# Nine steps of an attention and gated-MLP kernel moved in a hand-listed order: one small load, one copy, three PE steps and four others of batches 0 and 1

## The chip, the core and the metric

The kernel runs on one NeuronCore of a Trainium2 chip. The core has five engines with instruction queues of their own, each worked off in order: TensorE (PE, matrix products), VectorE (DVE), ScalarE (ACT), GpSimd (POOL) and SyncE (SP), which here only issues DMA transfers. The metric is the device time of one execution in microseconds (us), the median of several runs; less is better.

## The reference, cut to what matters

Eight batches, eight heads, 576 tokens, head size 64. A causal sliding-window attention (window 64) is followed by a gated MLP with a spatial projection over the tokens.

```python
scores = scale * np.matmul(q, k.transpose(0, 1, 3, 2))
mask = (rel >= 0) & (rel < window)                 # rel = query - key, window 64
attn = softmax(np.where(mask, scores, -1e9))
x = (attn @ v) as [batch, token, head * 64]        # 512 columns
h = np.maximum(x @ w_in, 0.0)                      # 1024 columns: u and v halves
v_n = (v - mean) / sqrt(var + 1e-6)                # over the 512 columns of v
v_s = einsum('ts,bsd->btd', w_spatial, v_n) + b_spatial
out = (u * v_s) @ w_out
```

## The kernel before

The whole program is a list of 1117 named steps. The functions `load_steps`, `value_steps`, `att_steps`, `gmlp_steps` and so on only describe the steps; the text `ORDER` says in which order they are issued, on which engine, and which PSUM bank or which buffer of a pool each new tile takes (`S1_0:PE:4:7:1:2` is a step on PE that takes banks 4, 7, 1 and 2). Nothing else orders the work: each engine runs its steps in the order of the text and waits at a step for the steps that it depends on, and for the last readers of the bank or buffer that it takes.

A step's name begins with its kind and goes on with the batch `b` and, behind an underscore, the head group `g` (0 or 1) and a part. The kinds that matter here:

- `ldk`, `ldq`, `ldv`, `ldx`: loads of k, q and v (`ldv0_4` the last 64 tokens of v of batch 0, `ldx0_g` the rest of it). `ldwsp`, `ldwin`, `ldwo`, `ldb`: loads of the weights and the bias. `DQ` issues on SP at once; `DG` also on SP, but only when the last matmul listed ahead of it is done.
- `ck`, `cq`, `cv`, `cx`, `cwsp`, `cwin`, `cwo`: the casts of what was loaded to 16 bit (tiles hk, hq, hv, hx, wnat, win, wout). `tk`, `tq`: 32x32 transposes on DVE.
- `Y0_g` and `F0_gk` bring v of batch 0 into token order (tile hv, by way of PSUM). `sl` and `su` copy hv, shifted by 64 tokens, into the lower and upper half of tile hs; `s4` fills its last 64 tokens from the load. In the later batches they come in two parts, `sl1_0`, `su1_0`, `sl1_1`, `su1_1`.
- `S` scores (64 small matmuls), `E` the exponentials on ACT (`E1_10` and `E1_11` write the first tile e of group 1 of batch 1, `E1_12` and `E1_13` the second), `M` the mask on DVE (`M1_10` needs `E1_10` and `E1_11`; `M1_11` the other two), `Z` row sums, `N` and `n` their reciprocal by logarithm and exponential (tile lz), `P` the product with v (from hv and hs), `X` the scaling of it (tile x). `_r` is the remainder of 64 tokens.
- `W0` to `W4` transpose w_spatial on PE and need all five `cwsp`; `We` copy the results out. `V0a`, `V0b`, `V`: v half of the MLP; `Vr`, `Vb`, `Va` its relu and statistics; `L1`, `L2`, `A` the normalisation; `U`, `Ur` the u half; `G`, `Ge` the spatial product and the gate; `O`, `Oe`, `st` the output.

POOL's casts and copies are split into pieces (`cp`): `ck1_0` on POOL would be three, `su1_0` is two copies of 64x512, `cwo10` is one cast of 128x512.

Of the kernel before, what the change touches and what calls it, by code (L numbers as in the profile page):

```python
# [20 lines left out]
ldq0_1a:DQ:3 D9:PE:0 D10:PE:0 D11:PE:0 ck0_0b:ACT cx0_0:DVE:2 D12:PE:0 D13:PE:0 ldq0_1b:DQ D14:PE:0  # L21
ldk0_1b:DQ Y0_0:PE:0:1:2:3 cq0_0b:POOL F0_00:ACT:0 ldx0_1:DQ D15:PE:4 ck0_1a:POOL:3 tk0_0b:DVE
F0_01:ACT ldwsp0:DQ:4 D16:PE:4 D17:PE:4 ldwsp2:DQ:5 tq0_0a:DVE:1 F0_02:DVE D18:PE:4 tq0_0b:DVE
ldwsp1:DQ:6 ldwin10:DQ:7 ldv0_4:DQ D19:PE:4 F0_03:ACT D20:PE:4 cq0_1a:DVE:1 tk0_1a:DVE:2 D21:PE:4
cq0_1b:POOL tq0_1a:DVE:3 D22:PE:4 cwsp0:POOL ck0_1b:DVE ldwin11:DQ:0 tq0_1b:DVE D23:PE:4 D24:PE:4
D25:PE:4 S0_0:PE:4:5:6:7 E0_02:ACT:0 tk0_1b:DVE E0_03:ACT sl0_0x:ACT:0 E0_00:ACT:1 S0_1:PE:0:1:3:2
E0_01:ACT su0_0x:DVE M0_00:DVE cwin110:POOL ldq1_0:DG:1 cx0_1:ACT:2 E0_10:ACT:2 Y0_1:PE:6:7:4:5
ldk1_0:DG:3 M0_01:DVE Z0_01:PE:0 E0_12:ACT:3 F0_12:DVE E0_11:ACT F0_10:DVE cwin111:POOL
S0_r:PE:3:4:1:6 cwsp4:DVE E0_13:ACT E0_r0:ACT:0 M0_11:DVE ldwin01:DQ:2 Z0_00:PE:2 E0_r1:ACT
M0_10:DVE cwsp1:DVE E0_r2:ACT cwsp3:DVE F0_11:ACT cq1_0:POOL:0 cwsp2:DVE P0_00:PE:3 E0_r3:ACT  # L30
Z0_10:PE:4 N0_01:ACT:0 N0_10:ACT:1 Z0_11:PE:1 F0_13:ACT ldwin00:DQ:5 N0_00:ACT:2 M0_r:DVE P0_01:PE:7
W4:PE:6 W3:PE:0 sl0_1x:DVE cwin011:POOL n0_01:ACT su0_1x:DVE n0_00:ACT N0_11:ACT:3 P0_11:PE:4
n0_10:ACT cwin010:POOL cwin101:DVE Z0_r:PE:5 P0_10:PE:2 We3:DVE n0_11:ACT s40_:DVE X0_00:DVE:1
W1:PE:1 cwin100:ACT W0:PE:0 ldk1_1:DG:4 X0_01:DVE P0_r:PE:3 W2:PE:7 N0_r:ACT:4 cwin001:POOL
X0_10:DVE:2 ldq1_1:DQ:6 We4:DVE V0a_3:PE:5 We0:ACT X0_11:DVE ldb:DQ:7 V0a_2:PE:2 V0a_0:PE:0
ck1_0:ACT:1 We2:DVE tq1_0:DVE:4 V0b_2:PE ldwo0:DQ:0 tk1_0:DVE:5 We1:ACT V0b_3:PE n0_r:ACT V0a_1:PE:6
# [3 lines left out]
U0_4:PE:0 Va0_3:DVE E1_01:ACT ldv1_4:DG ck1_1:POOL:3 Vb0_4:DVE:4 Va0_0:DVE Va0_1:DVE Va0_4:DVE  # L40
cb:POOL tk1_1:DVE:0 U0_3:PE:5 L10:ACT:0 ldk2_0:DG:3 L20:ACT U0_1:PE:6 Ur0_4:ACT:0 A0_2:DVE:0
cq1_1:ACT:2 U0_0:PE:4 cwo00:ACT U0_2:PE:3 ldq2_0:DQ:2 A0_0:DVE:1 A0_4:DVE Ur0_1:ACT:1 Ur0_0:ACT:2
Ur0_3:ACT:3 ldq2_1:DQ:5 A0_3:DVE:2 A0_1:DVE:3 tq1_1:DVE:1 cwo01:POOL Ur0_2:ACT:4 G0_0:PE:1
S1_1:PE:2:7:0:6 M1_01:DVE E1_10:ACT:3 E1_11:ACT Ge0_0:DVE:0 E1_12:ACT:2 G0_3:PE:4 S1_r:PE:5:3:1:2
E1_r0:ACT:1 E1_13:ACT M1_00:DVE cv1_0:DVE:1 M1_10:DVE Z1_01:PE:7 sl1_0:POOL:1 N1_01:ACT:5 Z1_00:PE:0
Z1_10:PE:5 E1_r1:ACT G0_1:PE:6 cwo11:POOL G0_4:PE:7 ldk2_1:DQ:4 Ge0_3:DVE:1 G0_2:PE:4 N1_10:ACT:2
M1_11:DVE Z1_11:PE:3 N1_00:ACT:0 su1_0:POOL n1_10:ACT ldq3_0:DG:7 E1_r2:ACT s41_:ACT ldk3_0:DG:6
n1_00:ACT cv1_1:DVE Ge0_1:DVE:2 su1_1:DVE sl1_1:DVE cwo10:POOL ck2_0:POOL:0 P1_10:PE:5 ldv2_0:DQ:0
ldv2_1:DG N1_11:ACT:1 Ge0_2:DVE:3 P1_11:PE:0 n1_01:ACT n1_11:ACT cq2_1:POOL:1 X1_10:DVE:3 E1_r3:ACT
cq2_0:ACT:3 P1_00:PE:6 ck2_1:POOL:2 P1_01:PE:1 O0_2:PE:4 ldv2_2:DQ X1_00:DVE:0 Oe0_2:ACT:0 O0_0:PE:3  # L50
X1_11:DVE ldv2_3:DG tk2_0:DVE:2 O0_3:PE:5 O0_1:PE:6 Oe0_0:ACT:1 tq2_0:DVE:3 X1_01:DVE Oe0_3:ACT
S2_0:PE:2:0:4:3 Oe0_1:ACT V1_3:PE:5 Ge0_4:DVE:4 E2_00:ACT:3 V1_0:PE:1 tq2_1:DVE:0 E2_02:ACT:2
E2_01:ACT V1_2:PE:6 V1_1:PE:7 M1_r:DVE M2_00:DVE Vr1_3:ACT:5 E2_03:ACT tk2_1:DVE:1 Vr1_0:ACT:6
Vr1_2:ACT:7 P1_r:PE:2 cq3_0:POOL:0 Vr1_1:ACT:0 Z1_r:PE:4 S2_1:PE:0:5:3:1 ldv2_4:DQ U1_3:PE:6
N1_r:ACT:3 n1_r:ACT M2_01:DVE E2_12:ACT:1 Vb1_1:DVE:5 X1_r:DVE:1 E2_10:ACT:0 ck3_0:POOL:3 V1_4:PE:7
E2_13:ACT Ur1_3:ACT:5 Vb1_0:DVE:0 Z2_00:PE:4 Z2_01:PE:3 Vb1_3:DVE:1 Vr1_4:ACT:1 Vb1_2:DVE:2
Va1_3:DVE U1_4:PE:2 N2_01:ACT:4 Vb1_4:DVE:1 U1_1:PE:0 Va1_0:DVE cv2_0:POOL:0 N2_00:ACT:2 Va1_1:DVE
ldq3_1:DG:0 E2_11:ACT U1_2:PE:1 Va1_2:DVE Va1_4:DVE L11:ACT:1 M2_11:DVE M2_10:DVE sl2_0:POOL:0
Ur1_4:ACT:2 L21:ACT ldk3_1:DQ:1 S2_r:PE:6:3:4:5 Ur1_1:ACT:3 A1_4:DVE ldv3_0:DG:1 A1_3:DVE:4
E2_r0:ACT:0 A1_1:DVE:5 Z2_11:PE:2 Oe0_4:ACT:0 A1_0:DVE:6 Z2_10:PE:0 N2_10:ACT:0 A1_2:DVE:7 s42_:ACT  # L60
E2_r1:ACT U1_0:PE:6 G1_1:PE:7 N2_11:ACT:1 ldv3_1:DQ cv2_1:POOL su2_0:POOL Ur1_0:ACT:1 E2_r2:ACT
G1_4:PE:0 tq3_0:DVE:4 Ur1_2:ACT:4 G1_0:PE:3 tk3_0:DVE:5 Ge1_4:DVE:5 ldv3_2:DG ldq4_1:DG:3
Ge1_1:DVE:6 su2_1:POOL sl2_1:ACT ldq4_0:DQ:2 ldv3_3:DQ S3_0:PE:2:6:4:1 E2_r3:ACT Ge1_0:DVE:7
P2_10:PE:0 M2_r:DVE n2_10:ACT P2_00:PE:7 n2_11:ACT n2_00:ACT st0_4:DQ P2_01:PE:5 E3_00:ACT:0
X2_10:DVE:1 st0_0:DQ n2_01:ACT cq3_1:POOL:1 X2_00:DVE:2 E3_01:ACT ldk4_0:DG:5 P2_11:PE:3 X2_11:DVE
ck3_1:ACT:2 ldv4_0:DG:0 G1_2:PE:0 X2_01:DVE Ge1_2:DVE:8 P2_r:PE:2 tq3_1:DVE:0 Z2_r:PE:7 cv3_0:POOL:1
ldv3_4:DQ N2_r:ACT:5 n2_r:ACT E3_02:ACT:3 G1_3:PE:3 tk3_1:DVE:1 V2_1:PE:6 Vr2_1:ACT:4 Vb2_1:DVE:0
V2_2:PE:5 sl3_0:POOL:1 V2_3:PE:0 Vr2_2:ACT:2 Ge1_3:DVE:9 Vr2_3:ACT:3 S3_1:PE:7:4:6:5 X2_r:DVE:0
U2_1:PE:3 E3_03:ACT E3_10:ACT:2 Vb2_2:DVE:1 S3_r:PE:0:2:1:7 M3_00:DVE E3_12:ACT:1 su3_0:POOL
E3_r0:ACT:1 M3_01:DVE E3_13:ACT Vb2_3:DVE:2 V2_4:PE:6 Z3_00:PE:0 M3_11:DVE E3_r1:ACT Z3_01:PE:5  # L70
Ur2_1:ACT:0 V2_0:PE:2 cv3_1:ACT Va2_3:DVE cq4_1:POOL:0 sl3_1:POOL Vr2_0:ACT:1 tq4_1:DVE:2 Va2_1:DVE
Vr2_4:ACT:5 Vb2_0:DVE:0 E3_r2:ACT cq4_0:POOL:3 O1_2:PE:3 Vb2_4:DVE:2 E3_11:ACT E3_r3:ACT Va2_0:DVE
Va2_2:DVE Va2_4:DVE su3_1:POOL U2_4:PE:2 M3_r:DVE N3_01:ACT:3 L12:ACT:0 st0_1:DQ s43_:POOL
ldk4_1:DG:4 Oe1_4:ACT:0 L22:ACT M3_10:DVE ldv4_1:DQ Oe1_2:ACT:1 U2_0:PE:1 U2_2:PE:4 U2_3:PE:7
tq4_0:DVE:3 N3_00:ACT:0 O1_1:PE:5 A2_3:DVE:0 A2_4:DVE ldv4_2:DG Ur2_2:ACT:2 ldv4_3:DQ ldv4_4:DQ
A2_2:DVE:1 O1_3:PE:6 Ur2_4:ACT:3 A2_0:DVE:2 Z3_r:PE:3 A2_1:DVE:3 Z3_11:PE:0 Ur2_3:ACT:1 Ur2_0:ACT:4
P3_00:PE:4 n3_00:ACT Oe1_3:ACT N3_r:ACT:2 Z3_10:PE:2 P3_10:PE:7 X3_00:DVE:0 n3_01:ACT ck4_0:POOL:1
N3_10:ACT:1 P3_01:PE:1 tk4_0:DVE:0 P3_11:PE:6 O1_0:PE:3 G2_0:PE:4 N3_11:ACT:4 ldq6_1:DG:7 n3_10:ACT
G2_3:PE:2 n3_11:ACT cv4_0:POOL:0 n3_r:ACT X3_01:DVE X3_10:DVE:3 Oe1_0:ACT:0 sl4_0:ACT:0 X3_11:DVE
Oe1_1:ACT G2_1:PE:0 ck4_1:ACT:2 S4_0:PE:1:7:3:6 Ge2_3:DVE:0 E4_00:ACT:0 ldk5_0:DQ:6 E4_02:ACT:2  # L80
Ge2_0:DVE:1 V3_1:PE:2 E4_01:ACT Vr3_1:ACT:0 ldk5_1:DG:0 V3_2:PE:5 E4_03:ACT G2_2:PE:4 tk4_1:DVE:1
S4_1:PE:1:3:7:2 s44_:ACT Vr3_2:ACT:6 E4_12:ACT:3 su4_0:POOL U3_1:PE:6 E4_10:ACT:1 ldv5_0:DQ:1
E4_13:ACT st1_4:DQ V3_3:PE:5 E4_11:ACT Ge2_1:DVE:2 Vb3_1:DVE:0 ldq5_0:DG:1 U3_0:PE:0 M4_00:DVE
M4_01:DVE ldq5_1:DG:3 Ge2_2:DVE:3 cv4_1:POOL V3_0:PE:7 M4_11:DVE Vr3_3:ACT:7 G2_4:PE:1 M4_10:DVE
su4_1:POOL Ur3_0:ACT:5 st1_0:DQ Ur3_1:ACT:1 S4_r:PE:4:2:3:5 Vb3_2:DVE:1 Vb3_3:DVE:2 Vr3_0:ACT:3
ldq6_0:DQ:2 E4_r0:ACT:0 sl4_1:POOL ck5_1:POOL:0 E4_r1:ACT ck5_0:POOL:3 Z4_10:PE:0 P3_r:PE:6
Va3_3:DVE P4_10:PE:7 X3_r:DVE:1 Z4_00:PE:4 N4_10:ACT:5 E4_r2:ACT Z4_01:PE:2 n4_10:ACT Ge2_4:DVE:4
N4_00:ACT:0 P4_00:PE:6 ldv5_1:DQ N4_01:ACT:3 ldv5_2:DG P4_11:PE:0 V3_4:PE:3 cq5_0:POOL:1 tk5_1:DVE:4
Z4_11:PE:1 X4_10:DVE:1 n4_00:ACT P4_01:PE:4 U3_4:PE:2 E4_r3:ACT N4_11:ACT:1 Oe2_4:ACT:0 ldv5_3:DG
U3_2:PE:7 tk5_0:DVE:5 U3_3:PE:5 Va3_1:DVE X4_00:DVE:2 Vr3_4:ACT:5 n4_11:ACT Ur3_4:ACT:4 tq5_0:DVE:0  # L90
cq5_1:POOL:2 Ur3_3:ACT:0 O2_2:PE:1 n4_01:ACT S5_0:PE:6:3:2:5 Ur3_2:ACT:2 X4_11:DVE O2_3:PE:0
# [872 lines left out]
```

## Time and profile before

| | |
|---|---|
| runs timed | 199.40, 199.76, 199.78 us |
| median | 199.76 us |
| profiled execution, first to last instruction (span) | 197.1 us |
| what the timed runs have beside that span | 2.3 to 2.7 us |
| mean granted TensorE clock | 0.981 |
| busy: PE, DVE, ACT, POOL | 186.1, 162.7, 161.9, 83.7 us |

The page gives the profiled execution by its span alone; a time of its own, with what lies around the span, is not listed, so it is set against the timed runs as above. Times in the profile count from the start of the span. In a row of the timeline the first number is the start, the second the length of the stretch from the first to the last of its instructions, then engine, line, operation, tiles and count; what stands in square brackets is how long the engine sat idle ahead of it and what ended the wait. "PEclk" or "clock" is the granted share of TensorE's full speed.

### The profile page before, as it was taken

How to read it: one execution, taken by the hardware profiler on the slowest of the kernel's cores; microseconds unless marked ns; L12 is line 12 of the kernel's file. 1: busy time of each engine (PE TensorE's matmuls, PEld its weight loads, DVE VectorE, ACT ScalarE, POOL GpSimd, SP SyncE). 2: the span in 40 equal slices, each digit the busy share in tenths (PEclk: the TensorE clock that was granted, in tenths of full speed). 3: DMA queues.
4: the chain of work that ended last, by engine and by line, in shares of the span. 5: the costliest groups of instructions: out<-in, count | busy, mean ns of one | idle time of the engine just before them, and what ended most of it. 6: DMA issues, size and time to landing. Idle time of an engine off the chain costs nothing.

```text
span 197.1 us, 7044 instructions
## 1 busy us (share of the span) xinstructions
PE 186.1 (94%) x2935; PEld 98.1 (50%) x2935; DVE 162.7 (83%) x321; ACT 161.9 (82%) x342; POOL 83.7 (42%) x148
## 2 busy tenths in 40 slices
...
GB/s 196 386 319 310 389 395 239 277 399 294 125 141 259 232 367 300 152 249 226 266 309 325 303 228 156 118 307 199 191 7 97 172 3 0 30 40 161 135 169 191
DMA packets 46977, 42.67 MB, mean 217 GB/s; under 512 B 34529, under 2 KB 35681, under 8 KB 46946
## 3 DMA queue, kind: packets, MB, share of 16 engines
...
HBM read 32.79 MB, written 9.44 MB: 214 GB/s over the span
## 4 chain that ended last, share of the span: by engine, by line
PE 66%; ACT 19%; DVE 10%; issue 2%; POOL 1%
PE bank L295 66%; ACT e L568 6%; ACT vs L726 3%; ACT ru L828 3%; DVE e L573 2%; DVE x L605 2%; DVE g L859 1%; DVE hs L312 1%; ACT lz L612 1%; DVE vn L799 1%; ACT ob L703 1%; POOL hq L307 1%; DVE st L728 1%; DVE hv L312 1%; DVE qT L433 1%
## 5 line engine op out<-in xcount | busy, mean ns | idle before, releaser
L295 PE MATMUL bank<-wspT,vn 128*128 128x512 f16 (+3 forms) x320 | 43.1, 286 | 0.9 <-DVE vn L799 0.7
L295 PE MATMUL bank<-wout,g 128*128 128x512 f16 (+2 forms) x164 | 39.1, 375 | 0.3 <-DVE x L605 0.2
L295 PE MATMUL bank<-win,x 128*128 128x512 f16 (+1 forms) x160 | 38.6, 380 | 0.2 <-ACT e L568 0.2
L568 ACT ACTIVATE e<-bank 128x512 f16<-128x512 f32 x64 | 35.3, 603 | 3.3 <-PE bank L295 3.2
L295 PE MATMUL bank<-x,win 128*128 128x64 f16 (+1 forms) x256 | 35.0, 286 | 0.0
L859 DVE TENSOR_TENSOR g<-bank,ru 128x512 f16<-128x512 f32 (+1 forms) x40 | 24.1, 623 | 11.7 <-PE bank L295 7.0
L728 DVE BATCH_NORM_STATS2 st<-vs 128x6 f32<-128x512 f16 (+1 forms) x40 | 26.4, 679 | 8.9 <-ACT vs L726 8.7
L310 POOL COPY hs<-hv 64x512 f16<-64x512 f16 x38 | 25.4, 694 | 13.6 <-ACT hv L303 8.1
L295 PEld LDWEIGHTS <-vn 128*128 128x128 f16 (+1 forms) x320 | 20.1, 97 | 20.2 <-DVE vn L799 2.0
L703 ACT COPY ob<-bank 128x512 f32<-128x512 f32 (+1 forms) x39 | 22.9, 593 | 8.2 <-PE bank L295 7.9
L726 ACT ACTIVATE vs<-bank 128x512 f16<-128x512 f32 (+1 forms) x40 | 23.5, 607 | 4.4 <-PE bank L295 4.3
L828 ACT ACTIVATE ru<-bank 128x512 f32<-128x512 f32 (+1 forms) x40 | 21.2, 561 | 3.5 <-PE bank L295 3.4
L573 DVE TENSOR_TENSOR e<-e,mask 128x1024 f16<-128x1024 f16 x32 | 22.4, 720 | 1.7 <-ACT e L568 1.5
L295 PEld LDWEIGHTS <-win 128*128 128x128 f16 x256 | 15.8, 98 | 15.4 <-issue 1.5
L295 PEld LDWEIGHTS <-x 128*128 128x128 f16 (+1 forms) x160 | 14.9, 100 | 16.5 <-issue 0.8
L295 PEld LDWEIGHTS <-g 128*128 128x128 f16 (+1 forms) x164 | 15.0, 100 | 14.5 <-issue 0.4
L605 DVE TENSOR_TENSOR x<-bank,lz 128x512 f16<-128x512 f32 x32 | 20.5, 673 | 1.0 <-ACT lz L614 0.9
L433 DVE STREAM_TRANSPOSE kT<-hk 128x576 f32<-128x576 f32 (+1 forms) x18 | 20.2, 1121 | 1.0 <-ACT hk L303 1.0
L433 DVE STREAM_TRANSPOSE qT<-hq 128x576 f32<-128x576 f32 (+1 forms) x18 | 20.1, 1118 | 0.8 <-POOL hq L307 0.5
L307 POOL CAST hq<-nq 128x384 f16<-128x384 f32 x30 | 14.1, 505 | 14.9 <-DMA nq<-in_q_dram 8.8
L614 ACT ACTIVATE lz<-lz 128x512 f32<-128x512 f32 x32 | 19.9, 649 | 0.0
L307 POOL CAST hk<-nk 128x384 f16<-128x384 f32 x30 | 15.9, 567 | 9.3 <-DMA nk<-in_k_dram 9.2
...
## 6 DMA issues: line engine op xcount, KB each, us to landing
...
ws<-in_moe_w_spatial_dram SPq DMA_DIRECT2D x2, 576.0 KB, 10.2
```

The costliest lines, as they stand in the source:

```text
L295: last[0] = nc.tensor.matmul(*a, **kw)
L307: nc.gpsimd.tensor_copy(o[:, n:n + w], i[:, n:n + w])
L310: nc.gpsimd.tensor_copy(o[:, c, :, :], i[:, c, :, :])
L433: lambda e, cs=cs, j0=j0, j1=j1: nc.vector.transpose(qt.t[:, :].rearrange("p (i j) -> p j i", j=18)[:, j0:j1, :], h.t[:, cs].bitcast(f32). ...
L568: lambda e, u=u, w=w: nc.scalar.activation(e2[u].t[:, w, :], sc[2 * u + w].t[:, :], AF.Exp, bias=0.0, scale=0.125),
L573: mins.append(add(f"M{b}_{g}{u}", ("DVE", 0.65), key, lambda e, u=u: nc.vector.tensor_tensor(e2[u].t[:, :, :], e2[u].t[:, :, :], mask[:, : ...
L605: lambda e, u=u, ob=ob, lz=lz: nc.vector.tensor_tensor(x.t[:, u, :], ob.t[:, :], lz.t[:, :], ALU.mult),
L703: lambda e: (nc.vector.tensor_copy if last else nc.scalar.copy)(view(), m.t[rows, 0:n]),
L726: rl = add(f"Vr{b}_{j}", ("ACT", 0.49), key, lambda e: nc.scalar.activation(vs.t[0:jn, :], m.t[0:jn, :], AF.Relu), deps=[pv], acq=[vs], us ...
L728: s1 = add(f"Vb{b}_{j}", ("DVE", 0.6), key + 0.02, lambda e: nc.vector.bn_stats(st6.t[0:jn, 0:6], vs.t[0:jn, :]), deps=[rl], acq=[st6], us ...
L828: lambda e, m=m, ru=ru, n=n: nc.scalar.activation(ru.t[:, 0:n], m.t[:, 0:n], AF.Relu), deps=[pu], acq=[ru], uses=[m])))
L859: lambda e, m=m, g=g, ru=ru, n=n: nc.vector.tensor_tensor(g.t[:, 0:n], m.t[:, 0:n], ru.t[:, 0:n], ALU.mult),
```

## The change

The steps, engines and instructions stay the same ones. In the list these move:

1. `ldv0_4` from behind `ldwin10` to ahead of `ldwsp0`.
2. `sl0_0x` (ACT) from between `E0_03` and `E0_00` to ahead of `E0_02`.
3. `ldq1_0` and `ldk1_0` (both `DG`) from behind `S0_1` and `Y0_1` to behind `S0_r`; they stay next in SP's own order.
4. `N0_10` (ACT) behind `F0_13` and `N0_00`.
5. On PE, `W3` ahead of `W4`, `W1` ahead of `P0_11`, and `P0_r` ahead of `W0`. Thereby the `DG` load `ldk1_1`, listed behind `W0`, waits for `P0_r` where it waited for `P0_10` (transposes are not counted as matmuls there).
6. `s40_` (DVE) ahead of `cwin101` and `We3`.
7. In batch 1, `E1_12` (ACT) ahead of `E1_11`, and `cwo10` (POOL) ahead of `su1_0`.

Beside it 278 of the 290 PE steps take other banks, and some lz and st buffers are numbered anew. The code gets a helper `wide` that, for a step on PE, issues the same matmul as before, and `out_steps` copies by `cp`, which issues the same copy on the engine that the list names.

```diff
-Y0... F0_01:ACT ldwsp0:DQ:4 D16:PE:4 D17:PE:4 ldwsp2:DQ:5 ... ldwsp1:DQ:6 ldwin10:DQ:7 ldv0_4:DQ
+ldv0_4:DQ F0_01:ACT ldwsp0:DQ:4 D16:PE:4 D17:PE:5 ldwsp2:DQ:5 ... ldwsp1:DQ:6 ldwin10:DQ:7
...
-... E1_10:ACT:3 E1_11:ACT Ge0_0:DVE:0 E1_12:ACT:2 ...
+... E1_10:ACT:3 E1_12:ACT:2 Ge0_0:DVE:0 E1_11:ACT ...
...
+    def wide(e, o, w, x, **kw):
+        if e == "PE":
+            mm(o[:, :], w, x, **kw)
+        else:
+            for f in (0, 64):
+                mm(o[f:f + 64, :], w[:, f:f + 64], x, **kw)
...
-        cpy = add(f"Oe{b}_{j}", ("DVE", 0.4) if last else ("ACT", 0.49), key,
-                  lambda e: (nc.vector.tensor_copy if last else nc.scalar.copy)(view(), m.t[rows, 0:n]),
+        cpy = add(f"Oe{b}_{j}", [("ACT", 0.49), ("DVE", 0.6)], key,
+                  lambda e: cp(e, view(), m.t[rows, 0:n]),
```

SP, the loads of the first microseconds: `ws` are `ldwsp0`, `ldwsp2` and `ldwsp1`, `wi` the w_in loads, the 64x8x64 `nv` is `ldv0_4`. Before:

```order
L489 DMA nv_131<-in_v_dram 128x4x256
L353 DMA ws_200<-in_moe_w_spatial_dram 128x2x576
L358 DMA ws_204<-in_moe_w_spatial_dram 64x576
L353 DMA ws_211<-in_moe_w_spatial_dram 128x2x576
L336 DMA wi_213<-in_moe_w_in_dram 128x2x512
L530 DMA nv_131<-in_v_dram 64x8x64
L336 DMA wi_230<-in_moe_w_in_dram 128x2x512
```

After:

```order
L496 DMA nv_131<-in_v_dram 128x4x256
L537 DMA nv_131<-in_v_dram 64x8x64
L360 DMA ws_201<-in_moe_w_spatial_dram 128x2x576
L365 DMA ws_205<-in_moe_w_spatial_dram 64x576
L360 DMA ws_212<-in_moe_w_spatial_dram 128x2x576
L343 DMA wi_214<-in_moe_w_in_dram 128x2x512
L343 DMA wi_232<-in_moe_w_in_dram 128x2x512
```

The small load went ahead of the three w_spatial loads and one w_in load; the rest keeps its order.

ACT in the middle of batch 1, behind the relus `Ur0` (tile ru): `e_1_10` is the tile that `M1_10` masks, `e_1_11` that of `M1_11`. Before:

```order
L828 ACTIVATE ru_2_845<-bank_70 128x512
L568 ACTIVATE e_1_10_919<-bank_69 128x512
L568 ACTIVATE e_1_10_919<-bank_74 128x512
L568 ACTIVATE e_1_11_924<-bank_67 128x512
L642 ACTIVATE er_965<-bank_72 128x128
L568 ACTIVATE e_1_11_924<-bank_73 128x512
```

After:

```order
L834 ACTIVATE ru_2_845<-bank_74 128x512
L575 ACTIVATE e_1_10_919<-bank_72 128x512
L575 ACTIVATE e_1_11_921<-bank_69 128x512
L575 ACTIVATE e_1_10_919<-bank_71 128x512
L649 ACTIVATE er_965<-bank_68 128x128
L575 ACTIVATE e_1_11_921<-bank_67 128x512
```

The second exponential of tile e_1_10 now comes third instead of second.

POOL in the same stretch: `hs` are the pieces of `sl1_0` (one) and `su1_0` (two), `wout_115` is `cwo10`. Before:

```order
L312 CAST wout_114<-wo_639 128x512
L310 COPY hs_975<-hv_969 64x512
L312 CAST wout_116<-wo_666 128x512
L310 COPY hs_975<-hv_969 64x512 x2
L312 CAST wout_115<-wo_666 128x512
L307 CAST hk_0_1048<-nk_0_800 128x384 x3
```

After:

```order
L319 CAST wout_114<-wo_639 128x512
L317 COPY hs_975<-hv_969 64x512
L319 CAST wout_116<-wo_666 128x512
L319 CAST wout_115<-wo_666 128x512
L317 COPY hs_975<-hv_969 64x512 x2
L314 CAST hk_0_1048<-nk_0_800 128x384 x3
```

Two weight casts now run in a row ahead of the two copies into hs.

265 lines of the change are left out of this document (132 added, 133 removed).

## The prediction

> **What bounds the kernel now.** I read the page first, then the chain of waits in order of time, then the timeline and the table of stretches of the first 48 us, which is all that the change reorders.
>
> ```profile
> span 197.1 us, 7044 instructions
> ...
> PE 186.1 (94%) x2935; PEld 98.1 (50%) x2935; DVE 162.7 (83%) x321; ACT 161.9 (82%) x342; POOL 83.7 (42%) x148
> ...
> PE 66%; ACT 19%; DVE 10%; issue 2%; POOL 1%
> ```
>
> PE is busy for 94% of the span and carries two thirds of the chain; DMA does not stand in it. So a delay that reaches the dense part near 42 us has little to swallow it later, while work saved at the start counts only if what ends last there moves too. The stretches of the start (busy time of PE, PEld, DVE, ACT, POOL, then clock, DMA share, GB/s):
>
> ```profile
> 8.00:12.00 4.00, 2.44 (x72) 1.24 (x70) 4.00 (x9) 1.59 (x4) 1.73 (x3) 1.00 1.06 385
> 12.00:16.00 4.00, 2.33 (x114) 1.74 (x114) 3.13 (x7) 4.00 (x8) 0.67 (x1) 0.94 1.05 307
> 16.00:20.00 4.00, 3.71 (x76) 2.49 (x54) 3.73 (x9) 3.49 (x12) 0.00 (x0) 0.50 1.11 295
> 20.00:24.00 4.00, 4.00 (x65) 2.89 (x64) 3.97 (x9) 3.47 (x8) 1.80 (x4) 0.71 1.01 391
> ```
>
> The DMA engines are busy throughout (share 1.01 to 1.11): loads land as the queue serves them, whenever they were issued. The clock is 0.50 in the third stretch; from 0.94 and 0.71 in its neighbours (0.24 and 1.16 us lost, so 0.5 and 2.3 us at half speed) the slow phase runs from 15.5 to 22.3 us. Where the start ends:
>
> ```profile
> 23.37 1.41 POOL L307 CAST hq<-nq 128x384 f16<-128x384 f32 x3 [0.32 <-DVE wspT L312]
> 24.79 1.15 ACT L303 CAST hk<-nk 128x1152 f16<-128x1152 f32 x1 [1.32 <-POOL hq L307]
> 24.82 1.26 DVE L433 STREAM_TRANSPOSE qT<-hq 128x576 f32<-128x576 f32 x1 [0.52 <-POOL hq L307]
> 27.29 0.80 PE L295 MATMUL bank<-qT,kT 32*64 32x128 f16 x64 [0.25 <-DVE kT L433]
> 28.96 1.41 POOL L307 CAST hk<-nk 128x384 f16<-128x384 f32 x3 [0.36 <-DMA nk<-in_k_dram]
> ```
>
> ACT sat idle 1.32 us ahead of `ck1_0`. The name in the bracket is another tensor's cast; by the code `ck1_0` reads only what `ldk1_0` brings, so I read this as the load landing. DVE (0.52) and PE (0.25) idle there too. This is a wall: work done sooner ahead of it waits at it, and lateness ahead of it is forgiven up to these three amounts. Behind it the chain:
>
> ```profile
> 35.37 0.66 DVE g L859
> ...
> 41.06 0.75 DVE hs L312
> 41.81 0.14 issue
> 41.95 5.43 PE bank L295 x120
> ```
>
> From 35.37 to 41.8 DVE runs without a gap (`Ge0_0` to `sl1_1`), then PE is released for 5.43 us of dense work. A delay of DVE in here is a delay of the kernel.
>
> **The change part by part, first the start.**
>
> ```profile
> 8.31 0.41 DVE L312 CAST hv<-bank 128x256 f16<-128x256 f32 x1
> 10.54 1.08 ACT L568 ACTIVATE e<-bank 128x512 f16<-128x512 f32 x2 [2.41 <-PE bank L295]
> 11.51 0.82 ACT L303 COPY hs<-hv 64x768 f16<-64x768 f16 x1
> 14.51 0.67 POOL L312 CAST wnat<-ws 128x576 f16<-128x576 f32 x1 [3.78 <-DMA ws<-in_moe_w_spatial_dram]
> 17.41 1.34 DVE L312 CAST wnat<-ws 128x576 f16<-128x576 f32 x3
> 18.68 0.42 DVE L646 TENSOR_TENSOR er<-er,maskr 128x512 f16<-128x512 f16 x1
> 18.85 1.50 PE L384 MATMUL bank<-id,wnat 128*64 128x128 f16 x10
> ```
>
> `sl0_0x` (11.51, 0.82 us; the next exponential starts 0.72 later) needs `F0_02`, which ends at 8.72 on DVE, and now fits into ACT's idle 2.41 us. ACT's next six steps come 0.7 us sooner, and `Y0_1`, `S0_r` and the Z and P steps with them.
>
> `ldv0_4` goes past four loads. Its price is read from the microsecond in which its packets ran before (16.75 to 17.75), and the landing of `ldwsp1` from its issue:
>
> ```profile
> DMA packets 549, 0.25 MB, mean 250 GB/s; under 512 B 485, under 2 KB 485, under 8 KB 549
> L353 SPq DMA_DIRECT2D ws<-in_moe_w_spatial_dram x1: 445/445/445, 7.7 to 7.7; - x1
> DMA to landing us min/median/max: 10.2/10.2/10.2
> ```
>
> The 64 large packets of 2 KB there are worth 0.13 MB / 385 GB/s = 0.34 us, so 485 small ones took 0.66 and all 512 take 0.7 us (by bytes alone 0.34; at most the full 1 us). The three w_spatial loads and `ldwin10` land that much later; `ldwin11` and all behind it stay, since what is ahead of them is the same. `ldwsp1` landed at 7.7 + 10.2 = 17.9, just where DVE's `cwsp3` (second of the three at 17.41) began; it and `cwsp2` shift to 18.6 and beyond, and with them `M0_r`, `X0_00` and `X0_01`. PE, which went straight from `P0_01` into the transposes at 18.85, now waits for `cwsp2` until about 19.45. What is left at the wall: DVE 0.7 late against 0.52 idle, +0.2; PE 0.6 late at half clock, of which work pushed behind 22.3 us regains half, so 0.3 against 0.25. The first matmuls of batch 1 come 0.1 to 0.2 late, ACT not at all until `Vr0_4`. Bounds: 0 (the load at its bytes' price) and 0.5 (1 us).
>
> The swaps `W3`/`W4`, `W1`, `P0_r`, `s40_`, `N0_10` keep the count of each engine's work ahead of the V steps and cost nothing by themselves; DVE's and PE's idle above covers them. `ldq1_0` and `ldk1_0` are issued 1 to 2 us later, `ldk1_1` with the SP queue behind it (`ldq1_1`, `ldb`, `ldwo0`) about 1.2 us later, behind `P0_r`. The cover is the backlog of the saturated queue: `ldk1_1`, issued at 21.6, was used only at 28.96. Gone, it would cost what the issue is late, 1.2 us at most. The new banks leave every release ahead of its taker by the same steps; `wide` and `cp` issue the same instructions.
>
> **Batch 1: the two swaps.**
>
> ```profile
> 35.77 1.57 ACT L568 ACTIVATE e<-bank 128x512 f16<-128x512 f32 x3 [0.41 <-PE bank L295]
> 36.55 0.67 DVE L312 CAST hv<-nv 128x1024 f16<-128x1024 f32 x1
> 37.15 0.67 DVE L573 TENSOR_TENSOR e<-e,mask 128x1024 f16<-128x1024 f16 x1
> 37.28 1.01 POOL L310 COPY hs<-hv 64x512 f16<-64x512 f16 x1 [4.65 <-DVE hv L312]
> 38.24 1.85 POOL L312 CAST wout<-wo 128x512 f16<-128x512 f32 x1
> 40.16 0.61 POOL L310 COPY hs<-hv 64x512 f16<-64x512 f16 x1
> 40.23 0.81 DVE L312 COPY hs<-hv 64x1024 f16<-64x1024 f16 x1
> 40.71 0.81 POOL L310 COPY hs<-hv 64x512 f16<-64x512 f16 x1
> 41.59 0.68 POOL L312 CAST wout<-wo 128x512 f16<-128x512 f32 x1
> 12.39 0.42 DVE L312 COPY hs<-hv 64x1024 f16<-64x1024 f16 x1
> ```
>
> *`E1_12` ahead of `E1_11`.* The three exponentials end at 37.34; `E1_11` was the second (36.86) and is now the third. `M1_10` started at 37.15 straight behind `cv1_0` and must now wait until about 37.39: DVE +0.24 in its gapless stretch. The 0.1 to 0.2 us from the start vanish in this wait, since the exponentials hang on the scores `S1_1`, for which ACT waited 0.41 us. `E1_13` keeps its place, so `M1_11` gains nothing.
>
> *`cwo10` ahead of `su1_0`.* `P1_10` reads hs: its release at 41.95 followed `sl1_1` (41.80) on DVE, and `su1_0` on POOL had ended at 41.52, 0.28 earlier. Now `cwo10` (0.68) runs first, and `cwo11` ahead of both ends with DVE's `cv1_1`, so 0.24 later. `su1_0` ends at 41.52 + 0.24 + 0.68 = 42.44, which is 0.64 behind the old 41.80: `P1_10` is now released by POOL, at about 42.6. `cwo10` gains nothing by being early: the O steps that need it started at 42.95 behind the P steps. Bounds: +0.24 (the cast slips into a stretch where POOL would have waited; DVE's own shift remains) and +1.4: DVE's copies stretch from 0.42 to 0.81 when POOL copies beside them and POOL's 0.6 to 1.85 beside DVE's masks and casts, so a cast that waits out two DVE copies takes 0.61 + 2 x 0.42 = 1.45, and 0.24 + 1.45 - 0.28 = 1.41. I take 0.64, by the cast's own row in the same place.
>
> **Sum**: start 0, exponentials and POOL together +0.64. The span becomes 197.7; what lies around it (2.7 us to the median) is untouched, so the median goes from 199.76 to 200.4.
>
> **The rivals.**
> 1. *Only DVE's shift remains, or slack near 48 us eats the rest*: up to +0.3, 200.0, no measurable change. For it: POOL idles elsewhere. Against: `su1_0` had just 0.28 to spare.
> 2. *Faster: the wall moves.* The queue ran at 307 and 295 GB/s from 12 to 20 us against 385 before; if, with the small packets gone from its middle, it regains these, loads land 4 x (78 + 90) / 385 = 1.75 us sooner, of which ACT's idle admits 1.32: -1.32 + 0.64 = -0.7, 199.1. It decides from 1.04 on. Against it: the dip at 12 to 16 holds no small packets.
> 3. *POOL comes first.* `sl1_0` starts at 37.28, ahead of the delayed `M1_10`; if DVE then waits until the copy has run its 0.61, to 37.89, DVE is 0.7 late and the release comes at 42.6 to 42.9: +0.65 to +0.9, 200.5 to 200.7. For it: cwo11's 1.85 shows that these two exclude each other; unknown is who wins. [...]
> 4. *The half clock stays.* PE gets an idle of 0.6 us ahead of `W3` (19.45 against 18.85). If the slow phase (6.8 us) lasts half as long again, to 25.7, about 1.3 us of the V steps runs at half speed and the transposes ahead of them too: they end 1.5 us later, 1.25 beyond PE's 0.25: 201.2 to 201.6. [...]
>
> **How the numbers follow.** Likeliest, 0.47: 200.4, its own range 200.0 to 201.2 by the bounds. Rival 1: 0.2. Rival 2: 0.17. Rivals 3 and 4: 0.08 each. Leaving out most of rival 2 and rival 4, not more than 0.2, the range is 199.3 to 201.2. A change of 0.2% (0.4 us) is about what can be told from none: slower by more holds nine tenths of the likeliest and rivals 3 and 4, less some doubt, 0.55; faster 0.18; the same 0.27.
>
> **What would show it.** Right: ACT's copy hs at 8.8; `wnat` casts near 18.6 and PE idle ahead of the first transpose; `ck1_0` still at 24.8 behind an idle; `M1_10` at 37.4; POOL's copies hs ending near 42.4, and PE's wait ahead of 42.6 released by POOL. Wrong: `ck1_0` at 24 or sooner; `P1_10` still released by DVE near 42.0; clock 0.5 beyond 22.3; or the delay present at 47 us and gone at 150.

## The result, and the profile after

The changed kernel takes 201.79 us (median; 200.65 to 202.46) against 199.76 for the kernel before, measured beside it: a ratio of 1.0102, 95% interval 1.0077 to 1.0127, so 1.5 to 2.5 us slower. Slower was forecast; 200.4 and a range to 201.2 were too little. Times given here are medians of all runs; the ratios, their intervals and the means further down leave out the few runs that were more than 1.5% above the fastest of the same kernel. The profiled execution has a span of 200.0 us and a time of 201.79. In nearly all runs with a span on record the time lies 1.7 to 1.9 us above it, so the profiled execution of before, with its 197.1, was one of about 198.9 us, some 0.9 below its median: the two profiles lie further apart (2.9) than the medians (2.0). The page, in the lines that answer to those shown of before:

```profile
span 200.0 us, 7035 instructions
...
PE 188.4 (94%) x2935; PEld 98.9 (49%) x2935; DVE 163.0 (82%) x321; ACT 163.1 (82%) x342; POOL 79.6 (40%) x148
...
PE 69%; ACT 12%; DVE 9%; DMA 6%; issue 2%; SPq 0%
```

The span is 2.9 us longer, PE busy 2.3 us more with the same 2935 matmuls: part of them ran at a lower clock for longer (mean granted clock 0.966 against 0.981). The stretches of the start (PE, PEld, DVE, ACT, POOL, clock, DMA share, GB/s):

```profile
12.00:16.00 4.00, 2.83 (x85) 1.77 (x86) 3.19 (x7) 3.78 (x7) 0.00 (x0) 0.61 1.07 258
16.00:20.00 4.00, 2.91 (x70) 1.88 (x66) 3.16 (x9) 3.17 (x11) 0.67 (x1) 0.50 1.05 381
20.00:24.00 4.00, 4.00 (x67) 3.10 (x63) 3.57 (x9) 3.32 (x7) 2.05 (x4) 0.50 1.02 394
24.00:28.00 4.00, 4.00 (x19) 1.79 (x18) 4.00 (x7) 2.85 (x5) 2.27 (x6) 0.68 1.03 369
```

The half clock, 15.5 to 22.3 us before, lasts from 12.9 to 26.6 here: 13.65 us in place of 6.83 by the clock's own records. Single steps of that stretch, from the timelines of ACT, DVE and PE:

```profile
9.24 0.83 ACT L310 COPY hs<-hv 64x768 f16<-64x768 f16 x1 [0.70 <-DVE hv L319]
16.88 0.45 DVE L319 CAST wnat<-ws 64x576 f16<-64x576 f32 x1 [0.84 <-DMA ws<-in_moe_w_spatial_dram]
17.26 1.28 DVE L580 TENSOR_TENSOR e<-e,mask 128x1024 f16<-128x1024 f16 x2
18.17 0.27 PE L295 MATMUL bank<-e,hv 128*64 128x64 f16 x3 [1.02 <-issue]
24.94 1.16 ACT L310 CAST hk<-nk 128x1152 f16<-128x1152 f32 x1
29.32 0.77 PE L295 MATMUL bank<-qT,kT 32*64 32x128 f16 x64
```

The copy `sl0_0x` sits in ACT's idle at 9.24, as said. It began 0.4 later than forecast, as the whole start did (`Y0_0` at 6.98 against 6.57). Little of its gain came through: `Y0_1` begins at 14.21 against 14.29, since the cast `cx0_1` ahead of it waited 0.22 us for the load `ldx0_1`, which landed at 13.09 in place of 12.19. The wall held: the load `ldk1_0` landed at 24.71 in both, and `ck1_0` begins at 24.94 against 24.79. But `S1_0`, which ended the start at 27.29 before, begins at 29.32, and this time PE itself is late, straight out of the V steps (25.00 to 29.38) that ran at half clock to 26.6. Ahead of this PE sat idle for 1.02 us at 17.15 inside `P0_00`, "issue" in the bracket: it waited for nothing that the profile shows. Then the middle of batch 1, DVE, ACT and POOL:

```profile
38.10 0.67 DVE L319 CAST hv<-nv 128x1024 f16<-128x1024 f32 x1
38.93 1.10 DVE L580 TENSOR_TENSOR e<-e,mask 128x1024 f16<-128x1024 f16 x1 [0.16 <-ACT e L575]
40.55 1.05 DVE L580 TENSOR_TENSOR e<-e,mask 128x1024 f16<-128x1024 f16 x1
41.52 1.10 DVE L319 CAST hv<-nv 128x1024 f16<-128x1024 f32 x1
...
37.32 1.57 ACT L575 ACTIVATE e<-bank 128x512 f16<-128x512 f32 x3
...
38.83 0.60 POOL L317 COPY hs<-hv 64x512 f16<-64x512 f16 x1 [6.42 <-DVE hv L319]
39.39 1.66 POOL L319 CAST wout<-wo 128x512 f16<-128x512 f32 x2
41.12 1.97 POOL L317 COPY hs<-hv 64x512 f16<-64x512 f16 x2
...
44.73 0.22 PE L295 MATMUL bank<-e,hs 128*64 128x64 f16 x2 [0.91 <-DVE hs L319]
```

`M1_10` (38.93) waits for the exponential, by 0.16 us, and is then 1.10 long in place of 0.67, to 40.03; `M1_11` takes 1.05 and `cv1_1` 1.10, also for 0.67. Before, all of DVE's masks and casts here took 0.67 and POOL's steps were the long ones (1.01, 1.85). `Ge0_0` begins 1.56 us later than before, `S2_0`, the first PE step behind the P and O steps, 2.79 us: 1.23 us were lost between these two. The release of `P1_10`, at 44.73, came from DVE's last copy, not from POOL, whose copies had ended at 43.09. The last step ends 2.78 later, so what is lost by then stays lost.

### The profile page after: what moved, and what is told of

The parts are those of the page before. It is cut to its first block, busy times and chain, and to the rows that moved or that the text cites. A ratio compares the mean times of both kernels' runs of the same rounds, so it can differ in the third digit from the quotient of the medians.

```text
span 200.0 us, 7035 instructions
## 1 busy us (share of the span) xinstructions
PE 188.4 (94%) x2935; PEld 98.9 (49%) x2935; DVE 163.0 (82%) x321; ACT 163.1 (82%) x342; POOL 79.6 (40%) x148
## 4 chain that ended last, share of the span: by engine, by line
PE 69%; ACT 12%; DVE 9%; DMA 6%; issue 2%; SPq 0%
PE bank L295 67%; DMA nv<-in_v_dram 6%; ACT e L575 3%; ACT ru L834 2%; DVE st L734 2%; PE bank L391 2%; ACT vs L732 2%; DVE e L580 1%; DVE g L865 1%; ACT lz L619 1%; DVE hv L319 1%; ACT ob L310 1%; DVE vn L805 1%; DVE x L612 1%; DVE qT L440 1%
## 5 line engine op out<-in xcount | busy, mean ns | idle before, releaser
L295 PE MATMUL bank<-win,x 128*128 128x512 f16 (+1 forms) x160 | 39.4, 385 | 0.3 <-DVE x L683 0.2
L317 POOL COPY hs<-hv 64x512 f16<-64x512 f16 x38 | 24.9, 679 | 17.3 <-ACT hv L310 10.0
L310 ACT COPY ob<-bank 128x512 f32<-128x512 f32 (+1 forms) x39 | 22.9, 594 | 8.7 <-PE bank L295 8.4
L580 DVE TENSOR_TENSOR e<-e,mask 128x1024 f16<-128x1024 f16 x32 | 23.3, 749 | 1.2 <-ACT e L575 1.1
L314 POOL CAST hq<-nq 128x384 f16<-128x384 f32 x30 | 14.1, 505 | 15.5 <-DMA nq<-in_q_dram 11.2
L619 ACT ACTIVATE lz<-bank 128x512 f32<-128x512 f32 x32 | 18.5, 609 | 1.9 <-PE bank L295 1.9
```

Source lines behind the costliest of these rows:

```text
L295: last[0] = nc.tensor.matmul(*a, **kw)
L310: nc.scalar.copy(o, i)
L317: nc.gpsimd.tensor_copy(o[:, c, :, :], i[:, c, :, :])
L580: mins.append(add(f"M{b}_{g}{u}", ("DVE", 0.65), key, lambda e, u=u: nc.vector.tensor_tensor(e2[u].t[:, :, :], e2[u].t[:, :, :], mask[:, : ...
L619: a = add(f"N{tag}", ("ACT", 0.06 + 0.00083 * n), key, lambda e: nc.scalar.activation(lz.t[:, 0:n], zb.t[:, 0:n], AF.Ln), deps=[z], acq=[l ...
```

## The experiments

Time is read in two ways: by the runs, against the kernel before on the same chip, and inside a profile by how much later than before a step begins. From `Ge0_0` to `S2_0` this second reading repeats to a few hundredths where that stretch is unchanged, while the start varies by more than a microsecond from one execution to the next. Theory A puts the loss on two causes: the early load, by late casts and PE's idle to a longer half clock, and POOL's steps shutting out DVE's in batch 1. Its rivals are named in each expectation.

**The load back in its place** (of the changed kernel).

```diff
-ldv0_4:DQ F0_01:ACT ldwsp0:DQ:4 ... ldwin10:DQ:7
+F0_01:ACT ldwsp0:DQ:4 ... ldwin10:DQ:7 ldv0_4:DQ
```

> Theory A (the load): ldv0_4 ahead of the w_spatial loads makes cwsp4 late, cwsp4 stands ahead of the masks M0_11 and M0_10 on DVE, PE idles 1.02 us inside P0_00, and this idle makes the half clock last two windows of 3.4 us longer. With the load back behind ldwin10: cwsp4 near 15.9, no idle of PE over 0.4 us between 16 and 19 us, half clock 6.8 us, S1_0 1.5 to 2 us sooner (27.3 to 27.8), time 200.0 to 200.7 against 201.8 for the changed kernel; the swaps of batch 1 keep their 0.6 to 1.2 us. Rival C (the length of the half clock hangs only on where its windows fall against the kernel's start, not on the change): half clock 10 to 14 us in most executions as in the changed kernel, time 201.3 to 201.8. Rival B (all of the loss is in batch 1): 201.6 to 201.9.

Measured: 201.19 us, ratio 1.0075 (1.0039 to 1.0112), above theory A's range and just short of rival C's. PE's idle in `P0_00` was still there, 1.22 us, with `cwsp4` at 16.57 and a half clock of 10.24; from `Ge0_0` to `S2_0` 1.23 us lost, as with the change. By the medians the load accounts for some 0.6 us; the intervals of the two ratios overlap, so this run alone does not show it. Theory A's way for it, the idle by the late cast, was wrong: the idle does not need the early load.

**The swaps of batch 1 back** (of the changed kernel).

```diff
-E1_10:ACT:3 E1_12:ACT:2 Ge0_0:DVE:0 E1_11:ACT
+E1_10:ACT:3 E1_11:ACT Ge0_0:DVE:0 E1_12:ACT:2
-N1_00:ACT:0 cwo10:POOL ... sl1_1:DVE su1_0:POOL
+N1_00:ACT:0 su1_0:POOL ... sl1_1:DVE cwo10:POOL
```

> The changed kernel with E1_11/E1_12 and su1_0/cwo10 in their old order. Theory B (POOL and DVE shut each other out in batch 1): M1_10 again 0.67 us long, the way from Ge0_0 to the release of P1_10 1.2 us shorter, time 0.6 to 1.2 us under the changed kernel's 201.8, so 200.6 to 201.2; half clock and S1_0 (29.3) as in the changed kernel. Rival: the batch 1 delay is slack that PE's later dense stretch swallows: 201.6 to 201.9.

Measured: 200.09 us, ratio 1.0025 (0.9996 to 1.0054). `M1_10` is 0.67 long again, and nothing is lost between `Ge0_0` and `S2_0` (+0.34 at both). Theory B, and more than it asked for; most of the loss is the swaps'. The half clock of the profile was 6.83 and `S1_0` at 27.67, not as in the changed kernel, though the start is the same one.

**Two fillers in PE's idle** (changed kernel, two more warm-up matmuls ahead of `P0_00`).

```diff
-P0_00:PE:2
+D26:PE:2 D27:PE:2 P0_00:PE:2
```

> The changed kernel with two more warm-up matmuls (128x512 on the scratch tile) on PE ahead of P0_00, in PE's idle of 1.02 us; all else as changed, the load still early. Theory A: PE has no idle over 0.4 us left there, half clock ends one or two windows of 3.4 us sooner (at 19.8 or 23.2 in place of 26.6), S1_0 0.8 to 2 us sooner, time 200.2 to 201.2. Rival C (idle of PE there plays no part): half clock as long as in the changed kernel, time 201.7 to 202.1. Rival D (the late load costs by itself, through DVE and PE's work, not through the clock): half clock shorter, but S1_0 within 0.4 us of 29.3 and the time within 0.4 us of 201.8.

Measured: 202.70 us, ratio 1.0152 (1.0121 to 1.0184); half clock 13.65 us as in the changed kernel, though no idle over 0.25 us is left there. A miss for theory A: this idle is not what makes the half clock long. The second filler began 0.79 us behind the first, and `P0_00`, now behind both, only at 19.73. The delay stayed at the 224th matmul of the program, which the second filler now is.

**The load alone** (of the kernel before).

```diff
-F0_01:ACT ldwsp0:DQ:4 ... ldwin10:DQ:7 ldv0_4:DQ
+F0_01:ACT ldv0_4:DQ ldwsp0:DQ:4 ... ldwin10:DQ:7
```

> The kernel before with ldv0_4 alone moved ahead of the w_spatial loads. Theory A: cwsp4 1.2 us later, PE idle about 1 us ahead of 18 us, half clock 10 to 14 us, S1_0 1 to 2 us later than 27.3, time 200.6 to 201.5 against 199.8. Rival B: 199.8 to 200.1. Rival C: half clock as before, 6.8 us, time 199.8 to 200.3.

Measured: 200.33 us, ratio 1.0033 (1.0006 to 1.0060): about 0.7 us, in the sense of theory A, but below its 200.6 and just above the 200.3 at which the rivals end, so the time does not decide between them; it differs from no change, narrowly. The profiled execution, one of the longest of this kernel, shows the long half clock:

```profile
16.00:20.00 4.00, 2.93 (x58) 1.55 (x58) 3.46 (x9) 2.43 (x9) 0.67 (x1) 0.50 1.03 360
20.00:24.00 4.00, 4.00 (x72) 3.18 (x69) 3.61 (x9) 4.00 (x9) 1.98 (x4) 0.50 1.02 398
24.00:28.00 4.00, 4.00 (x24) 1.81 (x22) 3.92 (x6) 3.02 (x6) 2.48 (x5) 0.50 1.03 400
```

**Each swap alone** (of the kernel before). The exponentials:

```diff
-E1_11:ACT Ge0_0:DVE:0 E1_12:ACT:2
+E1_12:ACT:2 Ge0_0:DVE:0 E1_11:ACT
```

> The kernel before with E1_12 ahead of E1_11 alone. Theory A (POOL's copy sl1_0 starts first and shuts DVE out): M1_10 ends 0.6 to 0.7 us later against Ge0_0 than before and is 1.0 to 1.1 us long in the trace, as in the changed kernel (1.10), and P1_10's release is 0.5 to 0.7 us later; time +0.5 to +0.7 on before. Rival B (only the late exponential counts): +0.24 at the release and in the time. Rival C (the cast's new place is what costs, this swap is hidden): 0 to 0.1.

The cast:

```diff
-su1_0:POOL n1_10:ACT ... sl1_1:DVE cwo10:POOL
+cwo10:POOL n1_10:ACT ... sl1_1:DVE su1_0:POOL
```

> The kernel before with cwo10 ahead of su1_0 alone. Theory A (each of the two swaps has its own share of the 1.24 us between Ge0_0 and the release of P1_10, by POOL's work shutting out cv1_1 and M1_11): +0.5 to +0.7 at the release and in the time. Rival B (the cast costs only as POOL's own delay, 0.68 against 0.28 of slack): su1_0 ends 0.4 us behind the old sl1_1, +0.4. Rival C (the shut-out needs both swaps together): 0 to 0.1 here and in the other kernel.

Measured: the exponentials 200.67 us, ratio 1.0081 (1.0051 to 1.0110), the cast 199.87 us, ratio 1.0015 (0.9991 to 1.0039). In the traces `Ge0_0` to `S2_0` grows by 0.97 us, more than theory A's 0.5 to 0.7, and by 0.27; together 1.24, and the kernel with both loses 1.23 (the agreement is in part luck, see below). The exponentials' swap alone, DVE and POOL:

```profile
36.83 1.10 DVE L568 TENSOR_TENSOR e<-e,mask 128x1024 f16<-128x1024 f16 x1 [0.16 <-ACT e L563]
39.05 1.10 DVE L307 CAST hv<-nv 128x1024 f16<-128x1024 f32 x1
...
36.73 0.60 POOL L305 COPY hs<-hv 64x512 f16<-64x512 f16 x1 [4.64 <-DVE hv L307]
37.29 1.11 POOL L307 CAST wout<-wo 128x512 f16<-128x512 f32 x1
38.46 2.16 POOL L305 COPY hs<-hv 64x512 f16<-64x512 f16 x2
```

POOL's copy runs 36.73 to 37.33, undisturbed, 0.60. DVE's mask starts 0.10 behind it, and its 1.10 is what was left of the copy, 0.50, and its own 0.6. Later the same again: `su1_0` starts at 38.46, sooner than before since the cast `cwo11` ahead of it took 1.11 in place of 1.85, and `cv1_1` waits in its turn. So a mask that is late by 0.23 us costs 0.97. Who starts first keeps its length here: the copy, 0.10 ahead, takes 0.60 and the mask 1.10; before, the mask, 0.13 ahead (37.15 and 37.28), took 0.67 and the copy 1.01. No row shown of before has POOL's copy ahead of a mask. The cast alone, DVE's and POOL's last copies:

```profile
40.79 1.45 DVE L307 COPY hs<-hv 64x1024 f16<-64x1024 f16 x2
...
41.27 1.44 POOL L305 COPY hs<-hv 64x512 f16<-64x512 f16 x2
...
42.77 0.22 PE L290 MATMUL bank<-e,hs 128*64 128x64 f16 x2 [0.50 <-POOL hs L305]
```

POOL ends at 42.71, 0.47 behind DVE, and releases `P1_10`: rival B, about, POOL's own lateness. With both swaps it is another way: DVE releases `P1_10` there, and against the exponentials' swap alone `M1_11` is 0.38 longer (1.05 for 0.67, beside POOL's second cast) and DVE's two copies together 0.11 shorter (1.35 for 1.46). These make 0.27, as much as the cast alone, by chance.

**The copy `sl1_0` on DVE** (changed kernel), behind `M1_10`, so that POOL has nothing ready when the mask is.

```diff
-M1_10:DVE Z1_01:PE:2 sl1_0:POOL:1
+M1_10:DVE sl1_0:DVE:1 Z1_01:PE:2
```

> The changed kernel with POOL's copy sl1_0 given to DVE right behind M1_10, so that POOL has no copy ready while M1_10 waits for E1_11. Theory A (POOL's copy, started first, shuts M1_10 out): M1_10 takes 0.67 us in the trace in place of 1.10, starts 0.2 to 0.3 behind cv1_0, and M1_11 starts no later than in the changed kernel though DVE has 0.25 to 0.42 us more to do. Rival B (M1_10 is long for another reason, the late exponential or its own operands): still 1.0 to 1.1 us. The time itself: 201.0 to 201.8, POOL's casts then starting sooner, with unknown effect behind.

```profile
38.53 1.10 DVE L314 CAST hv<-nv 128x1024 f16<-128x1024 f32 x1
39.55 0.68 DVE L575 TENSOR_TENSOR e<-e,mask 128x1024 f16<-128x1024 f16 x1
40.15 0.70 DVE L314 COPY hs<-hv 64x512 f16<-64x512 f16 x1
41.37 0.67 DVE L575 TENSOR_TENSOR e<-e,mask 128x1024 f16<-128x1024 f16 x1
...
37.42 1.66 POOL L314 CAST wout<-wo 128x512 f16<-128x512 f32 x2 [3.26 <-DMA wo<-in_moe_w_out_dram]
```

`M1_10` takes 0.68. The wait moved to the step that now meets POOL's casts (37.42 to 39.08): `cv1_0` is 1.10. From `Ge0_0` to `S2_0` 0.69 us are lost in place of 1.23, though DVE has a copy more. The time, 201.96 us (1.0092 to 1.0150) against 201.0 to 201.8 expected, does not show it; its start ran late by chance or on that chip (half clock over 10 us in all four runs). So the trace bears out theory A, the time neither way.

**Masks first** (changed kernel, swaps back, `cwsp4` behind `M0_10` on DVE).

```diff
-cwsp4:DVE E0_13:ACT ... M0_11:DVE ... M0_10:DVE
+E0_13:ACT ... M0_11:DVE ... M0_10:DVE cwsp4:DVE
```

> The changed kernel with the two swaps of batch 1 in their old order and, beside that, the weight cast cwsp4 behind the masks M0_11 and M0_10 on DVE; the load ldv0_4 stays early. To be held against the changed kernel with the swaps back alone, 200.1. Theory A (the early load costs by cwsp4 holding up the masks, and so PE, and so the clock): M0_10 ends near 17.5 in place of 18.5, PE's idle of 0.7 to 1.0 us inside P0_00 goes, half clock 6.8 us in most executions, time 199.5 to 199.8. Rival B (what is left against before lies elsewhere): 200.0 to 200.3 as without this move. Rival C: cwsp2 and W3, now later, open the same idle behind: 200.1 to 200.6.

Measured: 200.39 us, ratio 1.0058 (1.0038 to 1.0077), no better than without this move, with an idle of 0.87 us in `P0_00`. `M0_11` ended 1.17 us ahead of the matmul behind the idle. So the mask is not what `P0_00` waits for.

**Fillers in PE's early idle** (kernel before).

```diff
-S0_1:PE:0:1:3:2 ... Y0_1:PE:6:7:4:5
+D26:PE:0 ... D32:PE:0 S0_1:PE:0:1:3:2 ... D33:PE:6 ... D35:PE:6 Y0_1:PE:6:7:4:5
```

> The kernel before with seven warm-up matmuls (128x512 on the scratch tile) more on PE ahead of S0_1 and three more ahead of Y0_1, in PE's idle of 1.98 and 1.10 us. It asks what the half clock costs at all and whether PE's idle there brings it. Theory A (idle of PE brings the half clock, and its length counts): no half clock before 30 us, S1_0 0 to 0.5 us sooner than 27.3 (the wall at 24.8 holds), every execution near the fastest of before, 198.6 to 199.4, and a smaller spread. Rival B (such fillers don't count for the throttle): half clock as before, time 199.5 to 200. Rival C (the fillers run into S0_1 and Y0_1): 199.9 to 200.5.

Measured: 201.86 us, ratio 1.0125 (1.0103 to 1.0147). The half clock did shrink, to one stretch of 3.41 us in the profile and under 5.3 us in all in every run, so PE's early idle has to do with it. But the kernel lost 2 us, more than any expectation had; 0.94 of them are there at `S2_0` in the profile; where the rest arises is open. The 224th matmul now lies in `S0_r`, with an idle of 1.31 us ahead of it, and the 736th in `S2_0`, with 0.61. These two places gave the clue to the idle.

**The rest of the change** (load and swaps back) and **the copy `sl0_0x` alone** (on the kernel before), and **the kernel before again**.

```diff
 rest:  -ldv0_4, E1_11/E1_12, cwo10/su1_0 as changed
        +as before
 copy:  -E0_03:ACT sl0_0x:ACT:0 E0_00:ACT:1
        +sl0_0x:ACT:0 E0_02:ACT:0 tk0_1b:DVE E0_03:ACT E0_00:ACT:1
```

> The changed kernel with the load ldv0_4 back in its place and the two swaps of batch 1 back: only the copy sl0_0x, the moves of W3, W1, P0_r, s40_, N0_10 and the later ldq1_0, ldk1_0, ldk1_1 are left. Theory A (shares: swaps 1.24, load 0.4 to 0.6, the rest 0 to 0.3): +0.0 to +0.3 on before. Rival B (the rest has its own loss at the start, of the half clock, and the load none): +0.5 to +0.8. If the parts add, this and the load alone (+0.6) and the two swaps (+1.24) make up the whole change's 2.0.

> The kernel before with sl0_0x alone ahead of the first exponential. Theory A (the copy fits into ACT's idle and costs nothing): E0_00 0.4 us sooner, Y0_1 0 to 0.5 us sooner, ck1_0 still at its load, time 199.4 to 199.8 against 199.6, that is -0.2 to +0.2. Rival B (it lets PE run ahead into the half clock and the late instruction packet): half clock longer than 8.6 us in most executions, time +0.3 to +0.6.

> The kernel before once more, unchanged, to see how its own start varies from one execution to the next. Expected if the start's lateness in the other kernels is theirs: PE's idle at the matmul where every kernel of this case stalls (the second of P0_00, 223 matmuls into the program) 0.2 to 0.4 us, half clock 6.8 us, ck1_0 within 0.6 us of 24.8. Expected if it is this chip's variation: idle of 0.7 to 1.2 us there and a longer half clock here too. Time within 0.2 of before.

Measured: rest 199.65 us (0.9969 to 1.0016), copy 199.79 us (0.9972 to 1.0023), before again 199.61 us (0.9969 to 1.0020). The rest costs nothing that can be told. The parts add up: rest -0.07%, load 0.33%, the swaps 0.81% and 0.15%, sum 1.2%, whole 1.02%. The kernel before, profiled again, had an idle of 0.55 us at the 224th matmul (0.25 in the first profile), `S0_0` 0.45 us later and `ck1_0` at 24.73; three of its ten runs had a long half clock. So the start varies by itself, and single profiles of it prove little.

**Where the 224th matmul falls.** Each of the 26 warm-up matmuls became five short ones, so that the program is 104 matmuls longer and the 224th falls into `S0_1`; on the kernel before and on the changed one.

```diff
-            mm(m.t[:, :], scratch[:, 0:128], scratch[:, :], start=True, stop=True)
+            for n in range(5):
+                mm(m.t[:, 0:64], scratch[:, 0:128], scratch[:, 0:64], start=True, stop=True)
```

> The kernel before with each of the 26 warm-up matmuls (128x512) replaced by five of 128x64 on the same tile, which take about the same time (16 of this shape took 0.64 us at full clock, so five 0.2 against 0.215). The program is 104 matmuls longer, so the 224th, at which every kernel so far stood idle 1.4 to 1.6 us behind the end of PE's first instruction packet, now falls into S0_1, behind PE's wait of 2 us for q and k, in place of P0_00. Theory A (the idle ahead of P0_00's second matmul is the late packet, and it makes the half clock long): no idle over 0.2 us in P0_00, the resume in S0_1 again 1.4 to 1.6 us behind the packet's end and 0.2 to 0.5 us later than its start, half clock 6.8 us in nearly all executions, time 199.0 to 199.6 against 199.7. Rival B (the idle there is a wait for the mask M0_11): it stays 0.25 to 0.5 us, and the time is 199.6 to 199.8. Rival C (later packets now fall into other quick stretches, or the short matmuls bring the half clock sooner): 199.9 to 200.8, with a new idle at the 352nd or 480th matmul or an earlier half clock in the trace.

> The changed kernel with the same split of the warm-up matmuls. Theory A: the idle of 1.02 us inside P0_00 goes, half clock 6.8 us in most executions in place of 10 to 14, S1_0 1 to 2 us sooner in the trace, time 0.4 to 1.0 us under the changed kernel, 200.8 to 201.4; the 1.24 us of batch 1 stay. Rival B (the idle is a wait for M0_11, which hangs on cwsp4 and the load): idle 0.8 to 1.1 us there as before, time 201.6 to 202. Rival C: as in the kernel before with the split, 201.9 to 202.8.

Measured: 207.36 us (1.0321 to 1.0403) and 207.98 us (1.0295 to 1.0399): far slower than any expectation. Rival C's new idle times came, but they make up only part of it; what makes up the rest is open. `S0_1` began only at 13.80 and 14.45; the half clock lasted 17.07 and 13.65 us at the start, and 3.41 more from 105 us on. As to the cause of the idle they are plain all the same. The chain of waits of the kernel before with the split:

```profile
18.38 1.23 PE bank L290 x9
19.60 1.16 issue
20.76 0.48 PE bank L290 x9
...
102.86 2.20 issue
```

The changed kernel with the split, PE (the end of `P0_00`) and DVE (`M0_11`, `M0_10`):

```profile
18.60 0.32 PE L290 MATMUL bank<-e,hv 128*64 128x64 f16 x4
18.95 0.29 PE L290 MATMUL bank<-e,hv 128*64 128x64 f16 x2
...
18.60 1.28 DVE L575 TENSOR_TENSOR e<-e,mask 128x1024 f16<-128x1024 f16 x2
```

`P0_00` now runs through without an idle, and while the masks on DVE still run: it never needed them. The idle is at the 352nd matmul instead, 1.16 us in `P0_01`, which is 128 behind the 224th; and 2.20 us at the 1759th, one short of eleven times 128 further.

## Why the prediction was wrong, point by point

Two terms of the sum failed, by about the same amount: the exponentials' 0.24 (0.97 measured) and the start's 0 (0.5 to 0.7).

**The exponentials' swap: right mechanism for the lateness, wrong price.** "`M1_10` ... must now wait until about 37.39: DVE +0.24" held in the trace, 0.23. The term is mis-sized: 0.97 us. I took the lateness as the cost and the POOL copy that was due 0.13 us behind the old mask as one rival of 0.08. I had the row that said so, 37.28 for POOL's copy and 37.15 for the mask: any lateness over 0.13 changes who comes first. Rival 3 is what happened, the mask ending 0.66 later against the 0.7 that it gave, and its price also stopped too soon: once POOL runs undisturbed, its next steps meet DVE's next ones as well (`cv1_1` 1.10).

**The cast.** Forecast 0.40 beyond the 0.24; 0.27 alone, released by POOL as said. In the changed kernel that path failed: there DVE releases `P1_10`, 1.49 us behind the end of POOL's copies. Together 0.64 was forecast and 1.23 measured. That this lies inside the step's own bounds (0.24 to 1.4) is luck: the upper end was a cast on POOL that waits, and what took the time was DVE's masks and casts shut out by POOL.

**The start: the other step that failed** is "what is left at the wall", 0.2 to 0.3 us against 0.25, rounded to nothing. It took the half clock's end, 22.3, as given. The wall did hold; what passed it was PE itself, with V steps at half clock until 26.6. Rival 4 named this (25.7 and 1.25 us) with a chance of 0.08; that an idle of 0.6 us ahead of `W3` would bring it, no run shows. Measured by the runs it costs 0.5 us (the change with the swaps back, 1.0025) to 0.7 (the load alone). By the intervals the 0.5 could still be nothing (0.9996 to 1.0054); the 0.7 is just clear of it. The profiled pair shows 2.0 at `S1_0`, since the profile of before was a short half clock and that of after a long one.

**How the load comes into it is only half settled.** Its price was read from the packets of the queue, 0.7 us, at most 1; `cwsp4` came 1.26 later. Part of that arises on SP, which issues the loads one behind the other. Before, then after:

```profile
6.09 0.38 SPq L353 DMA_DIRECT2D ws<-in_moe_w_spatial_dram  x1
...
6.03 0.74 SPq L537 DMA_DIRECT2D nv<-in_v_dram  x1
7.37 0.42 SPq L360 DMA_DIRECT2D ws<-in_moe_w_spatial_dram  x1
```

The load just ahead of these rows went out at the same time in both (5.33 and 5.26), the issue of `ldv0_4` took 0.74 us, and the three w_spatial loads were issued 1.28, 1.16 and 1.15 later. In the seven profiles with the early load the first of them is issued at 7.37 to 8.49, in the nine others at 6.01 to 7.29; so the load's place counts, but one profile alone can't price it.

For what this costs, the runs are counted by their half clock. It is worked out from each run's mean clock and span, as twice the share of the clock that is missing times the span, and so has in it some half clock at the very end (0.7 us in the profile of before):

| start as in | runs counted | half clock, mean us | share over 8.8 us | mean time less the swaps' cost, us |
|---|---|---|---|---|
| before (with its repeats and the swaps alone) | 108 | 8.1 | 18% | 199.75 |
| before, copy alone | 12 | 8.9 | 33% | 199.87 |
| the rest (with and without swaps) | 21 | 10.1 | 67% | 199.78 |
| the load alone | 10 | 9.8 | 60% | 200.24 |
| after (with and without swaps) | 18 | 11.3 | 72% | 200.23 |

The swaps' cost is taken at 1.23 (both), 0.97 and 0.27 us. Over all 169 runs a microsecond more of half clock goes with 0.14 us more time, so the 3.3 us between the first and the last row would be 0.45 of the 0.48 us. But the rest has nearly as long a half clock and loses 0.03. The means of the rows with 10 to 21 runs are good to about 0.2 us (standard error). So the load costs about 0.5 us; that it does so by the clock alone is not shown, and why the half clock is longer with these starts isn't either: the fillers in `P0_00` closed the idle there and left it at 13.65, so the idle alone is not it.

**The idle in `P0_00`.** The prediction had PE idle ahead of `W3` for want of `cwsp2`; the idle came earlier and from elsewhere. In the records of DMA packets each profile has packets of 16 KB of instructions, which I read as PE's (23 of them, 0.38 MB, in the line `q8 instruction` of the page, before and after; 2935 matmuls are 22.9 times 128). In the fourteen profiles without the split, the 224th matmul starts 1.38 to 1.62 us behind the end of the first such packet, whatever step it belongs to, and 0.04 to 1.17 behind the end of `M0_11`. With the split of the kernel before, the 352nd starts 1.40 behind the end of the second packet; the 736th with the early fillers, 1.40, and the 1759th of the two split kernels, 1.41 and 1.47, start as far behind packets of theirs. That makes the late packet the cause; in the nine profiles with the load, the copy or the rest moved the packet began 0.87 to 1.41 us behind `Y0_1`, in the five with the start as before (fillers included) 0.25 to 0.40. Why is open; it is the one quantity of the start found here that separates the two groups without exception. The fillers put into this idle did not fill it: the second was itself the 224th matmul and began 0.79 us behind the first.

**What held**: the copy free of charge (0.9998), the moves of W3, W1, P0_r, the late loads at nothing (0.9993), the wall, the loss surviving to the end of the program (2.79 at 49 us, 2.78 at 195).

No version here beats the kernel before: undoing the swaps and the load gives 199.65, the same within its interval.
